# The last eight value blocks of the last attention head, as products of 32 stationary columns

## The chip, the cores and the metric

One core of one Trainium2 chip runs the whole program. The metric is the device time of one execution in microseconds. The kernel before takes 385.89 us, the median of 3 runs that lie between 385.88 and 386.0 us.

## The reference, cut to what matters

A decode step of one transformer block for 4 requests. A layer norm modulated by a condition feeds grouped-query attention over a cache of 4096 positions: 32 query heads on 8 key/value heads, so that 4 query heads share each cache. The result is projected, added to the input under a gate, normed and modulated again, and passes through a token-mixing MLP. All is 32-bit floating point.

```python
h = layernorm(x) * (1 + ca) + sa
q = (h @ wq).reshape(B, 1, 32, 128)             # B = 4 requests, one token each
scores = einsum("bhqd,bhkd->bhqk", q, k) / sqrt(128)
o = einsum("bhqk,bhkd->bhqd", softmax(scores), v)
x = x + ga * (o.reshape(B, 1, 4096) @ wo)
h = layernorm(x) * (1 + cb) + sb
x = x + gb * mixer_mlp(h)                       # w1, gelu, w2 over the token axis
```

## The kernel before, in words

The 4 requests times 8 key/value heads make 32 *heads*, numbered 0 to 31. Each has 2 MB of keys and 2 MB of values. One queue, SP's, loads them in order into a ring of three buffers; weights are loaded between them.

For each head the kernel forms the scores on TensorE, takes their maximum, exponentiates them on ScalarE, turns the result in 32 by 32 blocks on VectorE, and multiplies it with the values. The values of a head are 32 *blocks* of 128 positions by 128 channels. The turned weights `pT[:, j, :]` of block `j` are 32 columns, of which columns 0, 8, 16 and 24 belong to the four query heads and the others are padding.

A product on TensorE has a stationary operand, which is loaded first, and a moving operand, which streams through. In 32 bits each product is issued as two pairs of a weight load and a matmul. A stationary operand of 32 columns uses one of four *column groups* of the array, chosen by which 32 partitions of PSUM it writes; four products on the four groups can be under way together.

For the last heads `values_narrow` (line 294) takes the 32 weight columns as the stationary operand and a block of 128 channels as the moving one, block `j` on group `j % 4`. This leaves four partial sums in `pve`, query heads in rows and channels in columns. `copy_v` (line 311, step V31) brings them to SBUF as `po`, and `pick` (line 318, step a31) multiplies `po` with `eight`, a constant of four columns that adds the four groups, keeps the four real query heads and turns the result, so that channels lie on the partitions and the four heads in columns (`OT`).

Head 31 is split. Its first 30 blocks go that way. For its blocks 30 and 31 `values_turned` (line 305, step z31) takes the values themselves as 128 stationary columns and the four real weight columns as the moving operand; this gives the turned sum without a selection, in the same PSUM tile to which `pick` then adds the other 30 blocks.

`copy_o` (line 331, step A31) multiplies the sum with the inverse softmax sums into `both`. `project` (line 337, step p31) multiplies it with the output weights into `pgx`. Step I, ahead of it on TensorE, adds the gated residual `ep` to the same tile by a product with the 128-column identity. Between the second and third query head of step p31 `mean_last` sums up `tally`, which step j has made on VectorE. What follows is one chain: mean, variance, norm, 14 slices of the MLP and the output.

From head 23 on the order of the steps on every engine is written out by hand in `PLAN` (line 731). A step's letters name a function, its number the head, the digit after the point a part. `LV31` loads head 31's values in the pieces of `cuts` (line 729): blocks 0 to 15, 16 to 23, 24 to 27, 28 and 29, 30 and 31. `v31.0` to `v31.3` multiply them as they land, in the parts of `last` (line 730). Step f between them is a VectorE product of another tile, and step LW loads the last 1 MB of modulation weights behind all values; `zw0` uses them near the end.

Of the kernel before, what the change touches and what calls it, by code (L numbers as in the profile page):

```python
# [8 lines left out]
F32 = mybir.dt.float32  # L9
# [6 lines left out]
REP = HQ // HKV  # L16
NF = F // 128
EPS = 1e-5
P = 128
NS = B * HKV  # L20
# [8 lines left out]
def adaln_decode(ctx: ExitStack, tc: tile.TileContext, small, x, wmod, wq, kk, kv, vv, wo, out):  # L29
# [9 lines left out]
    ps_m = ctx.enter_context(tc.tile_pool(name="ps_m", bufs=2, space=PSUM))  # L39
    ps_e = ctx.enter_context(tc.tile_pool(name="ps_e", bufs=1, space=PSUM))  # L40
    ctx.enter_context(tc.manual_schedule())
    mm = nc.tensor.matmul
# [44 lines left out]
    eight = g32.rearrange("p (r x) -> p r x", x=8)[:, :, 0]  # L87
# [69 lines left out]
    KT, VT, WM = {}, {}, {}  # L157

    def slots():
        return ring.tile([P, 2, SK], F32, name="kv", tag="kv")  # L160
# [29 lines left out]
    def load_wm5():  # L190
        t = slots().rearrange("p s (k n) -> p (s k) n", n=D)
        nc.sync.dma_start(t[:, 0:4], wmod[2][:, 1])
        WM[5] = t[:, 0:4]
        return t[:, 4:6]

    def load_key(t, i):
        nc.sync.dma_start(t, kv[i - 2][:, 0])
        key(t, i)

    def load_v(t, i, cuts):  # L200
        value(t, i)
        src = (kv[i][:, 1] if i < NS - 2 else vv[i - NS + 2]).rearrange("p (j d) -> p j d", d=DH)
        for lo, hi in zip(cuts, cuts[1:]):
            nc.sync.dma_start(VT[i][:, lo:hi], src[:, lo:hi])
# [58 lines left out]
    def turn(i, halves=None):  # L263

        S.pop(i, None)
        if halves is None:
            dv.transpose(PL[i][0], PL[i][0])  # L267
            return
        for n in halves:
            p = PL[i][0][:, n * 512:(n + 1) * 512]  # L270
            dv.transpose(p, p)
# [22 lines left out]
    def values_narrow(i, ks, pv=None):  # L294
        if ks[0] == 0:
            PV[i] = ps_v.tile([P, DH], F32, name="pvn", tag="pv") if pv is None else pv
        pv = PV[i]
        pT = PL[i][0].rearrange("p (k r) -> p k r", r=32)
        top = 32 if i < NS - 1 else 30
        for k in ks:  # L300
            for j in range(4 * k, min(4 * k + 4, top)):
                c = j % 4
                mm(pv[32 * c:32 * c + 32, :], pT[:, j, :], VT[i][:, j, :], start=(k == 0), stop=(j + 4 >= top))  # L303

    def values_turned(i):
        pT = PL[i][0].rearrange("p (k r) -> p k r", r=32)
        OT[i] = pt = ps_m.tile([P, REP], F32, name="pt", tag="m")
        for j in (30, 31):
            mm(pt, VT[i][:, j, :], pT[:, j, 0:32:8], start=(j == 30), stop=False)

    def copy_v(i):
        pv = PV[i]
# [3 lines left out]
    ACC, OT = {}, {}  # L316

    def pick(i):
        po = PV.pop(i)
        n, m = po.shape[-1] // DH, WIDE.get(i, 1)  # L320
        if i in OT:
            mm(OT[i], po, eight, start=False, stop=True)
            return
        pt = ps_m.tile([P, m, REP], F32, name="pt", tag="m")
        OT[i] = pt[:, 0]
        for c in range(n):
            sel = sel4[:, c, :] if n > 1 else eight
            mm(pt, po[:, c * DH:(c + 1) * DH], sel.unsqueeze(1).to_broadcast([P, m, REP]),  # L328
               start=(c == 0), stop=(c == n - 1))
# [7 lines left out]
    def project(i, pa=None, between=None):  # L337
        b, h = divmod(i, HKV)
        oT = OT[i]
        if pa is None:  # L340
            pa = ps_m.tile([P, D], F32, name="pa", tag="m")
            for g in range(REP):
                mm(pa[32 * g:32 * g + 32, :], oT[:, g:g + 1].to_broadcast([P, 32]), wo_t[h][:, g, :],  # L343
                   start=True, stop=True)
        else:
            for g in range(REP):
                for c in range(4):
                    mm(pa[32 * c:32 * c + 32, :], oT[:, g:g + 1].to_broadcast([P, 32]),  # L348
                       wo_t[h][:, g, c * P:(c + 1) * P], start=(g == 0 and h == HKV - 2),
                       stop=(g == REP - 1 and h == HKV - 1))  # L350
                if between and g == 1:
                    between()
        PA[i] = pa
# [9 lines left out]
    def fold_groups(pool, acc, tag):  # L363
        pc = pool.tile([P, P], F32, name="pc", tag=tag)
        for c in range(4):
            mm(pc[32 * c:32 * c + 32, :], first, acc[:, c * P:(c + 1) * P], start=True, stop=True)
        return pc
# [215 lines left out]
    def fold_gate(gate, es):  # L583
        for e in es:
            w = wo_t[HKV - 2 + e // REP][:, e % REP]
            dv.tensor_tensor_reduce(w, w, gate, 1.0, 0.0, OP.mult, OP.add, rowsum[:, e:e + 1])
# [33 lines left out]
    def squares(x):  # L620
        flat = wk.tile([P, P], F32, name="flat")
        nc.scalar.activation(flat, x, AF.Square, bias=mu, accum_out=sq)
# [57 lines left out]
    for i in range(NS - HKV):  # L680
# [30 lines left out]
        if i == 2:  # L711
            for t in range(2, 5):
                pm = mod(t)
                dst = prep[:, {2: 1, 3: 2, 4: 3}[t]]
# [12 lines left out]
    pve = pgx = pc = ep = spare = slot = None  # L727
    gates = list(range(2 * REP))
    cuts = {NS - 1: (0, 16, 24, 28, 30, 32), NS - 2: (0, 16, 32)}
    last, halves = [(0, 1, 2, 3), (4, 5), (6,), (7,)], [(0, 1), (2, 3), (4, 5), (6, 7)]  # L730
    PLAN = """
    a23 v24.0 A23 p23 t25.0 P23 F R v24.1 LP25 G s26 t25.1 M H V24 LP26 Q a24 S26 v25.0 N s27 x A24 f p24 g
    x LP27 m26 S27 P24 m27 X26 X27 b26 B26 e26 x b27 v25.1 c g t26.1 l25 t26.0 B27 s28 V25 c g L25
# [1 line left out]
    LK30 t27.1 S29 P26 v27.0 m29 l27 g LK31 T t28.1 X29 LT t28.0 s30 L27 S30 b29 v27.1 B29 e29 l28 m30 V27  # L735
    LV28 L28 a27 g X30 t29.1 t29.0 l29 L29 s31 A27 LV29 b30 p27 x B30 S31 c c m31 e30 P27 X31 v28.0 f LT LV30
    b31 v28.1 B31 f e31 LV31 l30 V28 L30 t30.1 l31 L31 a28 t31.1 A28 p28 v29.0 v29.1 t30.0 f P28 V29 v30.0 a29
    v30.1 A29 LW p29 f v30.2 v30.3 t31.0 P29 g V30 Y y a30 A30 p30 E x v31.0 f v31.1 v31.2 v31.3 V31 z31 a31 I A31 j zy p31
    g T2 za zs zr zc0 zp0 zq zg zp1 zm zc1 T3 zn zw0
    """  # L740
    TABLE = {"s": scores, "S": row_max, "m": turn_max, "X": col_max, "b": spread_max, "B": copy_max, "e": expo,
# [4 lines left out]
    for step in PLAN.split():  # L746
        op, k = step.rstrip("0123456789."), step.lstrip("abcdefghijklmnopqrstuvwxyzABCDEFGHIJKLMNOPQRSTUVWXYZ")
        i, q = (int(n) for n in (k + ".0").split(".")[:2]) if k else (0, 0)
        if op in TABLE:
            TABLE[op](i)  # L750
        elif op in MIX:
            MIX[op]()
        elif op == "t":
            turn(i, [q])
        elif op == "v":
            if i < NS - 2:
                (values if i < NARROW else values_narrow)(i, range(4 * q, 4 * q + 4))
                continue
            if i == NS - 2 and q == 0:
                pve = ps_s.tile([P, 8, P], F32, name="pve", tag="s")  # L760
            values_narrow(i, (last if i == NS - 1 else halves)[q], pve[:, 4 * (NS - 1 - i)])
        elif step == "z31":
            values_turned(i)
        elif op == "p":
            project(i, pgx[:, 4] if i >= NS - 2 else None, mean_last if i == NS - 1 else None)
        elif op == "LT":
            slot = slots()
        elif op == "LK":
            load_key(slot[:, i % 2], i)
        elif op == "LV":  # L770
            load_v(slot[:, i % 2], i, cuts.get(i, (0, 32)))
        elif op == "LW":
            spare = load_wm5()
        elif op == "x":
            mix.expand(spare if mix.n == 6 else None)
        elif op == "f":
            fold_gate(gate, gates[:1])
            del gates[:1]
        elif step == "T":
            nc.scalar.activation(tab, neg1, AF.Exp)  # L780
        elif op == "Y":
            pgx = ps_s.tile([P, 8, P], F32, name="pgx", tag="s")
        elif op == "y":
            pc = fold_groups(ps_m, ACC.pop(B - 1), "m")
        elif op == "E":
            ep = cst.tile([P, P], F32, name="ep")
            dv.tensor_mul(ep, pc, prep[:, 1])
            dv.tensor_tensor_reduce(ep, ep, prep[:, 0], g32[:, 8 * (B - 1):8 * (B - 1) + 1], 0.0, OP.add, OP.add,
                                    tally[:, 0:1])
        elif op == "I":  # L790
            mm(pgx[:, 4], ident, ep, start=False, stop=False)
        elif step == "T2":
            nc.scalar.activation(tab, ones[0:1, 0:1], AF.Sqrt)
        elif step == "T3":
            nc.scalar.activation(tab, neg1, AF.Gelu_apprx_tanh)
        elif op == "za":
            al = centre(pgx[:, 4])
        elif op == "zs":
            squares(pgx[:, 4])
        elif op == "zr":  # L800
            products(al)
        elif op == "zp":
            if i == 0:
                ph = ps_s.tile([P, D], F32, name="ph3", tag="s")
            spread_last(ph, al, range(2 * i, 2 * i + 2))
        elif op == "zc":
            mix.fold_rest(i)
        elif op == "zg":
            pg = moments()
        elif op == "zm":  # L810
            variance(pg)
        elif op == "zn":
            hb, wr, br = affine_last(ph)
        elif op == "j":
            tally_up()
        elif op == "zw":
            modmm(pgx[:, 0], 5, (0,))
# [36 lines left out]
```

## Time and profile before

| | |
|---|---|
| median of 3 runs | 385.89 us |
| profiled execution, its own time | 385.9 us |
| its span, from first to last instruction | 384.1 us |
| TensorE matmul busy | 290.1 us (76%) |
| VectorE busy | 199.4 us (52%) |
| ScalarE busy | 111.9 us (29%) |
| DMA queue of the loads, share of 16 engines | 95.5% |
| read from memory | 157.32 MB, 410 GB/s over the span |

The engines are PE (TensorE matmul), PEld (TensorE weight load), DVE (VectorE), ACT (ScalarE), POOL (GpSimd) and SP (SyncE, which here issues loads). A row of the timeline has a start in us from the beginning of the span, a length, the engine, the line of the kernel, the operation, the tile written and those read, the shapes, and how many instructions of this kind follow each other (x8). Brackets at its end tell how long the engine was idle before and what released it. The length of a merged row goes from the first start to the last end. Ends of matmuls are modelled.

### The profile page before, as it was taken

What the parts mean: (1) busy time and instruction counts of PE and PEld (TensorE: products, weight loads), DVE (VectorE), ACT (ScalarE), POOL (GpSimd) and SP (SyncE); (2) the same over time, 40 slices, a digit from 0 to 9 for tenths busy, and PEclk for the clock granted to TensorE, in tenths of its full rate; (3) what the DMA queues carried; (4) which work ended last, traced back from release to release, by engine and by line L of the source; (5) the groups of instructions that cost most, each with busy time, mean ns of one, the idle gap of its engine ahead of it and who ended that gap; (6) DMA issues with size and microseconds to landing.
All of it is one profiled execution on the core that took longest, in us unless ns stands there. A gap on an engine that the chain in (4) does not pass through costs nothing.

```text
span 384.1 us, 5670 instructions
## 1 busy us (share of the span) xinstructions
PE 290.1 (76%) x2412; PEld 117.2 (31%) x2412; DVE 199.4 (52%) x414; ACT 111.9 (29%) x143; POOL 9.0 (2%) x34
## 2 busy tenths in 40 slices
PE   0958484973855928798777879988887887889984
PEld 0112121320222302234222223342222344333673
DVE  0130531440442714556666544657665567778777
ACT  1001210121110111113457310214675104757266
POOL 2100000000000000000000000000000000000000
PEclk9979956697896979989999995999999999999999
DMA  8999999999999999999999999999999999999930
GB/s 332 437 437 437 403 459 427 411 440 433 421 439 437 435 437 433 432 433 432 427 428 433 433 427 432 433 435 437 437 428 430 432 432 431 416 431 426 417 142 4
DMA packets 7410, 157.70 MB, mean 411 GB/s; under 512 B 964, under 2 KB 1236, under 8 KB 1496
## 3 DMA queue, kind: packets, MB, share of 16 engines
q1 hardware_dynamic: 7376, 157.33, 95.5%
q8 instruction: 19, 0.31, 0.3%
q14 instruction: 7, 0.06, 0.0%
q10 hardware_dynamic: 8, 0.00, 0.0%
HBM read 157.32 MB, written 0.01 MB: 410 GB/s over the span
## 4 chain that ended last, share of the span: by engine, by line
DMA 60%; PE 29%; DVE 8%; ACT 2%; issue 1%; POOL 0%; SPq 0%; DVEq 0%; ACTq 0%
DMA kv<-in_kv 58%; PE s L231 7%; PE pv L291 7%; PE s L122 3%; PE qs L138 2%; DVE p L267 2%; DVE m L236 2%; DMA sm<-in_small 2%; PE pa L343 2%; PE pt L328 2%; ACT wo L556 1%; PE pb L251 1%; PE pve L303 1%; PE pm L240 1%; PE pgx L348 1%
## 5 line engine op out<-in xcount | busy, mean ns | idle before, releaser
L231 PE MATMUL s<-kv,QT 128*32 128x512 f32 x512 | 71.8, 685 | 48.7 <-DMA kv<-in_kv 48.4
L236 DVE TENSOR_REDUCE m<-s 128x1 f32<-128x1024 f32 x32 | 39.2, 1224 | 100.7 <-PE s L231 100.7
L261 ACT ACTIVATE p<-s,nm 128x1024 f32<-128x1024 f32 x32 | 35.6, 1114 | 181.2 <-DVE nm L256 181.1
L291 PE MATMUL pv<-kv,p 128*32 128x512 f32 x464 | 67.8, 652 | 0.6 <-DMA kv<-in_kv 0.6
L231 PEld LDWEIGHTS s<-kv,QT 128*32 128x32 f32 x512 | 15.3, 119 | 91.0 <-DMA kv<-in_kv 62.9
L328 PEld LDWEIGHTS pt<-g,po 128*128 128x128 f32 x236 | 30.6, 202 | 27.6 <-issue 20.3
L343 PE MATMUL pa<-wo,oT 128*32 128x512 f32 x240 | 33.7, 633 | 4.9 <-DVE oT L335 4.7
L328 PE MATMUL pt<-g,po 128*128 128x4 f32 (+2 forms) x236 | 33.4, 265 | 1.5 <-DVE po L314 1.0
L267 DVE STREAM_TRANSPOSE p<-p 128x1024 f32<-128x1024 f32 x25 | 30.9, 1235 | 0.0
L314 DVE COPY po<-pv 128x512 f32<-128x512 f32 x29 | 20.0, 689 | 15.7 <-PE pv L291 15.6
L245 DVE TENSOR_REDUCE mx<-pm 1x128 f32<-1x512 f32 x32 | 21.3, 669 | 0.9 <-PE pm L240 0.9
L428 DVE TENSOR_SCALAR u<-hb,wr,sm 128x512 f32<-128x512 f32 x40 | 19.9, 540 | 1.9 <-POOL wr L423 1.0
L485 ACT ACTIVATE u<-u 128x1024 f32<-128x1024 f32 x20 | 20.4, 1052 | 1.5 <-DVE u L428 1.4
L261 ACT ACT_TABLE_LOAD x11 | 14.1, 1283 | 21.9 <-DVE nm L256 21.8
L361 DVE TENSOR_TENSOR acc<-acc,pa 128x512 f32<-128x512 f32 x26 | 17.8, 686 | 2.2 <-PE pa L343 2.1
L251 PEld LDWEIGHTS pb<-neg,mx 1*128 1x128 f32 x64 | 10.0, 194 | 27.6 <-DVE mx L245 25.9
L122 PE MATMUL s<-wm,sT 128*4 128x512 f32 x16 | 9.9, 788 | 10.4 <-POOL sT L108 10.4
L485 ACT ACT_TABLE_LOAD x13 | 16.7, 1283 | 0.2
L291 PEld LDWEIGHTS pv<-kv,p 128*32 128x32 f32 x464 | 13.6, 146 | 6.8 <-issue 2.8
L240 PE MATMUL pm<-ident,m 128*1 128x128 f32 x32 | 8.9, 280 | 7.6 <-DVE m L236 3.5
L251 PE MATMUL pb<-neg,mx 1*128 1x1 f32 x64 | 12.7, 265 | 2.1 <-DVE mx L245 2.1
L240 PEld LDWEIGHTS pm<-ident,m 128*1 128x1 f32 x32 | 2.5, 80 | 34.6 <-DVE rl L280 25.6
(173 smaller groups left out, 227.6 us busy)
## 6 DMA issues: line engine op xcount, KB each, us to landing
kv<-in_kv SPq DMA_DIRECT2D x28, 4096.0 KB, 22.0
wq<-in_wq SPq DMA_DIRECT2D x2, 4096.0 KB, 16.1
wo<-in_wo SPq DMA_DIRECT2D x4, 2048.0 KB
kv<-in_kv SPq DMA_DIRECT2D x4, 2048.0 KB, 21.1
wm<-in_wmod SPq DMA_DIRECT2D x2, 2048.0 KB, 16.1
kv<-in_kk SPq DMA_DIRECT2D x1, 4096.0 KB
kv<-in_vv SPq DMA_DIRECT2D x3, 1024.0 KB
wm<-in_wmod SPq DMA_DIRECT2D x1, 1024.0 KB
```

The lines of the kernel that those rows point to most:

```text
L122: mm(s0[0:B, t * D:(t + 1) * D], sT[:, k, :], wm01[:, t, k, :], start=(k == 0), stop=(k == 3))
L231: mm(s[32 * c:32 * c + 32, n * 512:(n + 1) * 512], QT[:, b, h, :], KT[i][:, (n * 4 + c) * 512:(n * 4 + c + 1) * 512], start=True, stop=True)
L236: dv.tensor_reduce(M[i], S[i], axis=AX.X, op=OP.max)
L245: dv.tensor_reduce(mx, M[i].rearrange("o (c r) -> o r c", c=4).unsqueeze(1).to_broadcast([1, 4, 32, 4]), axis=AX.X, op=OP.max)
L251: mm(pb, M[i].rearrange("o c r -> o (c r)"), neg1, start=True, stop=True)
L261: nc.scalar.activation(p, S[i], AF.Exp, bias=M.pop(i), accum_out=l)
L267: dv.transpose(PL[i][0], PL[i][0])
L291: mm(PV[i][32 * q:32 * q + 32, :], pT[:, 128 * k:128 * k + 128:4], VT[i][:, 4 * k:4 * k + 4, :].rearrange("p j d -> p (j d)"), start=(k < ...
L314: dv.tensor_copy(PV[i], pv)
L328: mm(pt, po[:, c * DH:(c + 1) * DH], sel.unsqueeze(1).to_broadcast([P, m, REP]), start=(c == 0), stop=(c == n - 1))
L343: mm(pa[32 * g:32 * g + 32, :], oT[:, g:g + 1].to_broadcast([P, 32]), wo_t[h][:, g, :], start=True, stop=True)
L485: nc.scalar.activation(u, u, AF.Gelu_apprx_tanh)
```

## The change

Head 31's narrow products now stop at block 23 instead of 29. Blocks 24 to 31 go through `values_turned`, and no longer with 128 stationary columns: each block's values are cut into four quarters of 32 channels, one for each column group, by the new function `quarters`. The four moving columns and the turned result stay as they were. The selection in `pick` is cut into quarters in the same way. In the order of steps the copy of the partial sums, V31, stands right behind the products of block 23. Then follow, all on TensorE, the products of blocks 24 to 27 (z31.0), the selection (a31), blocks 28 and 29 (z31.1), and blocks 30 and 31 (z31.2); step I and the rest follow as before. The loads and their pieces are unchanged.

```diff
-        top = 32 if i < NS - 1 else 30
+        top = 32 if i < NS - 1 else 24
...
-    def values_turned(i):
+    def quarters(dst, lhs, rhs, start, stop):
+        for c in range(4):
+            mm(dst[32 * c:32 * c + 32], lhs[:, 32 * c:32 * c + 32], rhs, start=start, stop=stop)
+
+    def values_turned(i, js):
         pT = PL[i][0].rearrange("p (k r) -> p k r", r=32)
-        OT[i] = pt = ps_m.tile([P, REP], F32, name="pt", tag="m")
-        for j in (30, 31):
-            mm(pt, VT[i][:, j, :], pT[:, j, 0:32:8], start=(j == 30), stop=False)
+        if js[0] == 24:
+            OT[i] = ps_m.tile([P, REP], F32, name="pt", tag="m")
+        for j in js:
+            quarters(OT[i], VT[i][:, j, :], pT[:, j, 0:32:8], j == 24, j == 31)
...
         if i in OT:
-            mm(OT[i], po, eight, start=False, stop=True)
+            quarters(OT[i], po, eight, False, False)
...
-    last, halves = [(0, 1, 2, 3), (4, 5), (6,), (7,)], [(0, 1), (2, 3), (4, 5), (6, 7)]
+    last, halves = [(0, 1, 2, 3), (4, 5)], [(0, 1), (2, 3), (4, 5), (6, 7)]
...
-    ... E x v31.0 f v31.1 v31.2 v31.3 V31 z31 a31 I A31 j zy p31
+    ... E x v31.0 f v31.1 V31 z31.0 a31 z31.1 z31.2 I A31 j zy p31
...
-        elif step == "z31":
-            values_turned(i)
+        elif op == "z":
+            values_turned(i, {0: range(24, 28), 1: (28, 29), 2: (30, 31)}[q])
```

More of the change, by code (lines that the diff above doesn't have):

```diff
@@ L737, in adaln_decode @@
     b31 v28.1 B31 f e31 LV31 l30 V28 L30 t30.1 l31 L31 a28 t31.1 A28 p28 v29.0 v29.1 t30.0 f P28 V29 v30.0 a29
-    v30.1 A29 LW p29 f v30.2 v30.3 t31.0 P29 g V30 Y y a30 A30 p30 E x v31.0 f v31.1 v31.2 v31.3 V31 z31 a31 I A31 j zy p31
+    v30.1 A29 LW p29 f v30.2 v30.3 t31.0 P29 g V30 Y y a30 A30 p30 E x v31.0 f v31.1 V31 z31.0 a31 z31.1 z31.2 I A31 j zy p31
     g T2 za zs zr zc0 zp0 zq zg zp1 zm zc1 T3 zn zw0
```

## The prediction

> **What bounds the kernel now.** I read the page first, for what sets the end at large.
>
> ```profile
> span 384.1 us, 5670 instructions
> DMA 60%; PE 29%; DVE 8%; ACT 2%; issue 1%; POOL 0%; SPq 0%; DVEq 0%; ACTq 0%
> q1 hardware_dynamic: 7376, 157.33, 95.5%
> ```
>
> The loads fill their queue nearly to the end, and the change touches none. So all it can win or lose lies between the landing of head 31's last values and the end, and I turned to the timeline there (stretches of it, by engine):
>
> ```profile
> 365.46 1.58 PEld L303 LDWEIGHTS pve<-kv,p 128*32 128x32 f32 x56
> 365.57 2.05 PE L303 MATMUL pve<-kv,p 128*32 128x128 f32 x60
> 366.14 0.69 DVE L586 CUSTOM_DVE_ANT_0 wo<-wo,gate 128x512 f32<-128x512 f32 x1
> 367.21 0.14 PEld L303 LDWEIGHTS pve<-kv,p 128*32 128x32 f32 x4 [0.17 <-DMA kv<-in_vv]
> 367.67 0.29 DVE L314 COPY po<-pve 128x128 f32<-128x128 f32 x1 [0.83 <-PE pve L303]
> 367.68 0.52 PEld L309 LDWEIGHTS pt<-p,kv 128*128 128x128 f32 x4 [0.33 <-PE pve L303]
> 367.71 0.58 PE L309 MATMUL pt<-p,kv 128*128 128x4 f32 x4
> 368.15 0.36 PE L322 MATMUL pt<-g,po 128*128 128x4 f32 x2
> 368.34 0.30 PEld L791 LDWEIGHTS pgx<-ep,ident 128*128 128x128 f32 x2
> 368.37 0.47 PE L791 MATMUL pgx<-ep,ident 128*128 128x128 f32 x2
> 368.55 0.16 DVE L335 TENSOR_TENSOR both<-pt,rl 128x4 f32<-128x4 f32 x1 [0.59 <-PE pt L322]
> 368.77 0.38 PEld L348 LDWEIGHTS pgx<-wo,both 128*32 128x32 f32 x16
> ```
>
> Blocks 0 to 23 run without a pause, as do 24 to 27 behind them; for blocks 28 and 29 TensorE waits for their piece until 367.21. For the last piece the instructions of line 309 have a row:
>
> ```profile
> L309 PE MATMUL pt<-p,kv x4: 245/252/253, 367.7 to 368.0; 128*128 128x4 f32 x4
> L309 PEldq EVENT_SEMAPHORE  x1: 51/51/51, 367.6 to 367.6; - x1
> ```
>
> TensorE's sequencer waits there, and the first product of block 30 follows at 367.68. The row names another releaser (the products of line 303, ended at 365.57 + 2.05 = 367.62), but this wait, done at about 367.65, is the later of the two. So the last values are there at **about 367.6**, and from then on everything is a chain on engines: 0.58 us of turned products, the selection until 368.15 + 0.36 = 368.51, step A31, and the projection at 368.77. The chain of waits tells what follows:
>
> ```profile
> 368.51 0.33 PE pgx L791 x2
> 368.84 0.56 PE pgx L348 x14
> 369.98 0.37 DVE a L617 x2
> 381.35 0.29 DVE osb L571
> ```
>
> All of it to the end hangs on the projection's first weight load, at 368.77. I cost the change by where this load goes.
>
> **The change part by part.** *The pace of four-group products* is the price on which all hangs, since 12 + 4 + 2 = 18 instructions become none, and instead eight blocks and a selection cost 9 x 4 x 2 = 72. The nearest row is `mean_last`, 32 stationary columns on four groups, with one moving column:
>
> ```profile
> 369.12 0.24 PEld L668 LDWEIGHTS pmu<-part,tally 128*32 128x32 f32 x8
> 369.23 0.22 PE L668 MATMUL pmu<-part,tally 128*32 128x1 f32 x8
> L668 PE MATMUL pmu<-part,tally x8: 167/168/170, 369.2 to 369.3; 128*32 128x1 f32 x8
> 369.26 0.38 PEld L348 LDWEIGHTS pgx<-wo,both 128*32 128x32 f32 x16
> ```
>
> Eight products of 0.17 us each end within 0.22, so they start within 0.05 of each other, 7 ns apart. A group's loads go ahead once the products of the group before have started: those of line 668's second group at 369.23, those of the next step (line 348) at 369.26. So a group of four costs **0.03 us**. The other bound is the pace with 128 moving columns:
>
> ```profile
> 365.46:366.87 1.41, 1.30 (x48) 1.33 (x48) 1.00 0.93 361
> ```
>
> This is line 303 alone in that window: 48 matmuls and loads, the loads busy for 1.33; a load takes 0.11 (next fence), so the 12 groups start (1.33 - 0.13)/11 = 0.11 us apart. I take 0.03, since four moving columns are nearer to one than to 128; the range keeps both.
>
> *The copy V31* moves ahead. Block 23's loads start at about 366.66 (11 groups of 0.11 after 365.46), its products one group later, at 366.79 with the four in a row, and they end 0.27 after (the length of a line 303 product, below), at 367.06. The copy came 0.05 after the end of its products (367.62, 367.67): now 367.11 to **367.40**. DVE is free, since line 586 ends at 366.83; were it not, the selection and the end would come as much later.
>
> ```profile
> L303 PEld LDWEIGHTS pve<-kv,p x60: 106/110/110, 365.5 to 367.2; 128*32 128x32 f32 x60
> L303 PE MATMUL pve<-kv,p x60: 272/273/297, 365.6 to 367.3; 128*32 128x128 f32 x60
> 363.68 0.29 DVE L314 COPY po<-pve 128x128 f32<-128x128 f32 x1 [0.33 <-PE pve L303]
> 364.03 0.30 PEld L328 LDWEIGHTS pt<-g,po 128*128 128x128 f32 x2 [0.46 <-DVE po L314]
> ```
>
> *z31.0.* Blocks 24 to 27 were multiplied right at 366.87 (the window holds exactly 24 blocks' 48 loads), so their piece was there. The step opens the tile `pt` and may need the extra wait instruction of line 309: start by 366.94. Eight groups of 0.03 end at 367.18, hidden behind the copy (0.52 until the selection can start, so up to 0.06 a group); without that cover the 0.24 would be on the path.
>
> *a31* is where a wait is added: it stands ahead of the last eight groups, and z31.1, z31.2, I and the projection queue behind it on TensorE. A selection loads 0.06 after its copy (363.97, 364.03): 367.46. Two groups: 367.52. *z31.1*, whose values came by 367.21, needs four groups, to 367.63; *z31.2*, whose values came at 367.6, four more: its last products start at **367.75** and, at 0.17 each, end at 367.92. The copy's path and the last load's (367.62 + 0.10) thus meet within 0.03; neither leaves room for more.
>
> *A31* started 0.04 after its products' end (368.51, 368.55), and the projection's load 0.22 after that: 367.96 and **368.18**. By this path alone 0.59 would be won.
>
> *Step I*, unchanged, comes into the way. It has 128 stationary columns between products of 32, and where the width changes, the trace shows loads that wait for no one else and yet start late:
>
> ```profile
> 298.78 0.43 PE L366 MATMUL pc<-yw,g 128*32 128x128 f32 x8 [0.83 <-DVE yw L501]
> 299.14 0.97 PEld L578 LDWEIGHTS pgb<-prep,ident 128*128 128x128 f32 x8 [0.20 <-issue]
> 371.37 0.69 PE L632 MATMUL ph<-a,ident 128*128 128x128 f32 x4
> 371.99 0.16 PEld L516 LDWEIGHTS pc<-u,sm 128*32 128x32 f32 x8
> ```
>
> Each starts 0.07 before the modelled end of the product ahead (299.21 and 299.14; 372.06 and 371.99). Before, this change of width lay ahead of block 30, under the wait for the last piece; now it lies ahead of I: its load starts at 367.92 - 0.07 = 367.85 (before, I came at the full pace of 0.11 behind the selection). From I's first load to the projection's were 368.77 - 368.34 = 0.43 us, and that too was bound by I: its products end at 368.84, 0.07 after. So the projection can load at **368.28**, 0.10 after `both` is ready. The wait moves from the selection to I.
>
> The sum: 368.77 - 368.28 = **0.49 us**. Behind it nothing has a fixed time that comes late. ACT's table is loaded by 368.82, before its use at 370.37 - 0.49; the last weights, issued at 357.69, land 12.3 later, at 370.0, before their use at 372.56 - 0.49.
>
> ```profile
> 357.69 0.33 SPq L192 DMA_DIRECT2D kv<-in_wmod  x1
> kv<-in_wmod SPq DMA_DIRECT2D x1, 1024.0 KB, 12.3
> 368.62 0.20 ACT L793 ACTIVATE tab<-ones 1x1 f32<-1x1 f32 x1
> 370.37 0.37 ACT L622 ACTIVATE flat<-pgx,mu 128x128 f32<-128x128 f32 x1 [1.55 <-DVE a L617]
> 372.56 0.24 PEld L209 LDWEIGHTS pgx<-kv,sT 128*32 128x32 f32 x8
> ```
>
> The profiled execution took 385.9 us, 1.8 more than its span, and the runs' median is the same 385.89: I forecast **385.4 us**, 385.2 to 385.6 with the roundings.
>
> **The rivals.** *The products are issued at 0.11 a group (slower).* The mechanism: each small product holds the array's entry for its own quarter of what a full one holds, whatever its moving columns. For it speaks line 309, also with four moving columns: four products in 0.58, 0.25 of it the last one's length, are 0.11 apart. Against it, that these have 128 columns to load, and line 668. Then z31.0 ends at 367.82, past the copy; ten groups more put the last products at 368.81 + 0.11, and the projection 0.53 later (0.17 - 0.07 + 0.43): 369.45, a loss of 0.68, **386.6 us**. It decides from a pace of 0.07 a group on: there the last products start at 368.24 and the projection at 368.77.
>
> For the same rival stands the Trainium skill, TensorEngine Tiling (Array Packing), section Instruction Overhead: every matmul carries about 60 cycles, so a small dimension is no place to gain by tiling; at the 2.4 GHz of its page TensorE: Matmul & The Clock Gate I estimate 25 ns a product, 0.10 a group, a loss of about 0.5 and 386.4. Line 668's products, 7 ns apart across four groups, disagree.
>
> *Half pace.* Line 668 shows only two groups in a row; over ten, load and product of a group could alternate instead of overlapping, 0.03 each: 0.06 a group, so the last products start at 368.03 and the projection at 368.56: a gain of 0.2, **385.7 us**. For it speaks only that no longer run is in the trace.
>
> *I does not wait for the array to empty,* as it did not behind the selection: then A31's path holds, 0.59, **385.3 us**. Against it are both rows on the change of width.
>
> *It is hidden anyway,* by something in the tail that keeps its own time: **385.9 us**. The rows of ACT and of the last weights speak against it, with 0.5 and 1.8 us of room.
>
> **How the numbers follow.** Forecast 0.58; no emptying ahead of I 0.12; half pace 0.10; hidden 0.07; 0.11 or 0.10 a group 0.10; something not seen 0.03. The largest gain that the last landing allows is 0.6 us, 0.16%, and 0.2%, about what a measurement of this kernel can tell from no change, is 0.77 us: all cases lie within it. Over it, at 385.1, I put 0.11 for a build whose loads end earlier by chance; below, beyond 386.7, 0.07, mostly from the slow pace. Within: 0.82. The range runs from 385.1 to 386.3: it takes in the forecast, the small rivals and the slow pace up to 0.09 a group; left out are its far end and the luck at either side.
>
> **What would show it.** Right: the copy at line 314 starts near 367.1; 32 loads of the turned products come ahead of the selection within 0.25; the last turned products start 0.1 to 0.2 after the last piece's landing; line 335 some 0.6 earlier against that landing; line 348 released by I and not by `both`, 0.5 earlier. Wrong: turned products 0.1 apart by group; a selection that waits on the copy past 367.5; an idle stretch ahead of line 348 that names DVE; a tail of other length than 15.3 us from line 348's first load to the end of the span.

## The result, and the profile after

| | before | after |
|---|---|---|
| median | 385.94 us (4 runs, 385.88 to 386.04) | 389.63 us (4 runs, 389.09 to 390.12) |
| ratio | | 1.0096, 95% interval 1.0081 to 1.0111 |
| profiled execution, span | 385.9, 384.1 us | 390.12, 388.3 us |

The change makes the kernel slower by about 1%, 3.7 us, where 0.5 us less was forecast. The profiled execution is the slowest of the four, so its profile accounts for 4.2 us and not for 3.7. The stretch that I had costed went nearly as forecast; the time was lost behind it. First the timeline of the changed kernel around the change (line numbers are 5 higher than before from line 314 on):

```profile
366.87 0.38 PEld L307 LDWEIGHTS pt<-p,kv 128*32 128x32 f32 x32 [0.15 <-issue]
367.05 0.29 DVE L319 COPY po<-pve 128x128 f32<-128x128 f32 x1 [0.29 <-PE pve L303]
367.40 0.16 PEld L307 LDWEIGHTS pt<-g,po 128*32 128x32 f32 x8 [0.15 <-DVE po L319]
367.45 0.37 PEld L307 LDWEIGHTS pt<-p,kv 128*32 128x32 f32 x32
367.85 0.30 PEld L796 LDWEIGHTS pgx<-ep,ident 128*128 128x128 f32 x2
367.98 0.16 DVE L340 TENSOR_TENSOR both<-pt,rl 128x4 f32<-128x4 f32 x1 [0.63 <-PE pt L307]
368.26 0.38 PEld L353 LDWEIGHTS pgx<-wo,both 128*32 128x32 f32 x16
368.75 0.16 PEld L353 LDWEIGHTS pgx<-wo,both 128*32 128x32 f32 x7
371.88 0.39 PEld L353 LDWEIGHTS pgx<-wo,both 128*32 128x32 f32 x9 [2.97 <-issue]
```

The projection's first load comes at 368.26, 0.51 earlier than before. But within its second half, after seven of sixteen loads, TensorE stands still for 2.97 us, and the profile names nothing that it waits for: "issue". The chain of waits has it on the path:

```profile
368.94 0.24 PE pgx L353 x7
369.18 2.70 issue
371.89 0.85 PE pgx L353 x9
```

Two sets of windows cut the end at the same instructions: the loads of head 30's projection, the first load of step p31, the load that comes late after the change, the first slice of the MLP (line 551, now 556), the end. The columns are the window, its length, busy time with instruction counts of PE, PEld, DVE, ACT and POOL, granted clock, share and GB/s of DMA. Before:

```profile
364.67:368.77 4.10, 4.01 (x101) 3.40 (x101) 2.59 (x10) 2.49 (x3) 0.00 (x0) 1.00 0.80 325
368.77:369.31 0.54, 0.54 (x29) 0.54 (x31) 0.54 (x3) 0.05 (x1) 0.00 (x0) 1.00 0.29 121
369.31:373.27 3.96, 3.71 (x88) 3.05 (x80) 2.97 (x14) 2.20 (x5) 0.76 (x2) 1.00 0.04 12
373.27:384.10 10.83, 5.04 (x136) 3.28 (x136) 8.07 (x19) 7.21 (x7) 0.00 (x0) 1.00 0.02 4
```

After:

```profile
364.59:368.26 3.67, 3.60 (x154) 3.23 (x154) 2.65 (x10) 2.07 (x2) 0.00 (x0) 1.00 0.83 333
368.26:371.88 3.62, 0.92 (x32) 0.65 (x31) 0.91 (x4) 0.48 (x2) 0.00 (x0) 0.90 0.17 70
371.88:377.47 5.59, 5.58 (x61) 4.81 (x65) 2.53 (x12) 2.20 (x5) 0.76 (x2) 0.50 0.01 3
377.47:388.30 10.83, 7.01 (x152) 4.72 (x144) 8.08 (x19) 7.21 (x7) 0.00 (x0) 0.82 0.02 4
```

Up to step p31: -0.51 (368.26 against 368.77), of which 0.08 was there before the change could act (head 30's projection at 364.59 against 364.67). The stretch with the pause: 3.62 for 0.54, +3.08. The norm behind it: 5.59 for 3.96, +1.63, at a granted clock of 0.50 instead of 1.00. The MLP and the output: 10.83 both times; in both kernels the chain runs through ScalarE for the first 6.7 us of it. The sum, +4.20, is the difference of the spans, 388.3 - 384.1.

What the pause waits for is told by the queues. The page counts q8, a queue of instructions, with 19 packets and 0.31 MB in both kernels: 16 KB each. Divided among them, TensorE's 2 x 2412 matmuls and loads of before are 254 a packet, so 256 instructions a packet is a likely size. In the changed kernel's DMA view, q8 moves nothing between 366 and 369.5 us, while the loads (q1) run; then comes one packet (columns: queue, packets, MB, share of 16 engines in a window of 0.1 us from 369.5 on):

```profile
q8 instruction: 1, 0.02, 58.8%
```

2.3 us later TensorE goes on, at 371.88. That made the **supply theory**: TensorE's instructions arrive in pieces of 256; the change has it use up one piece sooner than the next is there. Its rivals: the pause belongs to the place (step p31's second half, or the sums it needs; the *place theory*), to the turned products or to the new order.

### The profile page after: what moved, and what is told of

The parts are those of the page before. It is cut to its first block, busy times and chain, and to the rows that moved or that the text cites. A ratio compares the mean times of both kernels' runs of the same rounds, so it can differ in the third digit from the quotient of the medians.

```text
span 388.3 us, 5778 instructions
## 1 busy us (share of the span) xinstructions
PE 294.4 (76%) x2466; PEld 119.7 (31%) x2466; DVE 199.3 (51%) x414; ACT 111.9 (29%) x143; POOL 9.0 (2%) x34
## 4 chain that ended last, share of the span: by engine, by line
DMA 60%; PE 27%; DVE 8%; ACT 2%; issue 1%; POOL 0%; SPq 0%; ACTq 0%; DVEq 0%
DMA kv<-in_kv 58%; PE s L231 7%; PE pv L291 6%; PE s L122 3%; DVE m L236 3%; PE qs L138 2%; DVE p L267 2%; DMA sm<-in_small 2%; ACT wo L561 1%; PE pa L348 1%; PE pt L333 1%; PE pb L251 1%; PE pve L303 1%; PE pgx L353 1%; PE pm L240 1%
## 5 line engine op out<-in xcount | busy, mean ns | idle before, releaser
L291 PE MATMUL pv<-kv,p 128*32 128x512 f32 x464 | 66.5, 640 | 0.6 <-DMA kv<-in_kv 0.6
L348 PE MATMUL pa<-wo,oT 128*32 128x512 f32 x240 | 32.8, 618 | 5.0 <-DVE oT L340 4.8
L433 DVE TENSOR_SCALAR u<-hb,wr,sm 128x512 f32<-128x512 f32 x40 | 19.9, 540 | 1.9 <-POOL wr L428 1.0
```

The costliest lines, as they stand in the source:

```text
L291: mm(PV[i][32 * q:32 * q + 32, :], pT[:, 128 * k:128 * k + 128:4], VT[i][:, 4 * k:4 * k + 4, :].rearrange("p j d -> p (j d)"), start=(k < ...
```

## The experiments

Where a run is said to be shifted, products that make the first row of `prep` are repeated with the same result at the start of the program. Each is four instructions of TensorE, two loads and two matmuls:

```diff
+    for e in range(16):
+        c = e % 4
+        mm(px[32 * c:32 * c + 32, :], rows.rearrange("k b r -> k (b r)"),
+           xr[:, c * P:(c + 1) * P], start=True, stop=True)
```

### The changed kernel, shifted by 64 instructions

> The changed kernel, with 16 more of the small products that make the first row of prep (line 153, repeated, same result) at the start, where TensorE waits for loads: 64 instructions more ahead of everything that follows, nothing else. Supply theory: TensorE's instructions arrive in pieces of 256, and the pause of 2.97 us begins where a piece ends; then it begins 64 instructions earlier, at step I, ahead of the first load of step p31 and not within its second half; it still ends near 371.3 to 371.9 us, and the time stays at 389 to 390.5 us. Place theory: the pause belongs to step p31's second half (what it reads, or the sums that line 673 makes); then it stays between the seventh and the eighth load there, and the time at 389.6 us.

389.82 us (4 runs), ratio 1.0102 (1.0076 to 1.0127). The pause moved 64 instructions forward, to the middle of step I, in which no sum of step p31 is needed:

```profile
367.79 0.19 PEld L800 LDWEIGHTS pgx<-ep,ident 128*128 128x128 f32 x1
370.98 0.19 PEld L800 LDWEIGHTS pgx<-ep,ident 128*128 128x128 f32 x1 [3.00 <-issue]
```

A window from the start of the span to a moment within the pause counts what TensorE has begun by then. For the changed kernel:

```profile
0.00:371.00 371.00, 281.77 (x2261) 110.17 (x2261) 188.73 (x383) 102.51 (x131) 8.27 (x32) 0.91 0.99 425
```

For the shifted one:

```profile
0.00:370.00 370.00, 280.50 (x2261) 110.27 (x2261) 188.47 (x382) 102.64 (x131) 8.26 (x32) 0.92 0.99 426
```

Both stop after exactly **2261 matmuls and 2261 loads** (4522 instructions; the 4545 of the expectations counts 23 waits and the like with them). The place theory falls.

### The kernel before, shifted by 108 instructions

> The kernel before, with 27 more of the small products that make the first row of prep at the start: 108 instructions more, as many as the change adds, but none of the change. Supply theory: the piece that ended at 372.36 us in the kernel before now ends 108 instructions earlier, in the second half of step p31 at about 369.4 us, and the next is there some 5.8 us after the piece before it was finished (about 364.8): a pause of about 1.2 us, between 0.7 and 1.6, and a time of 386.7 to 387.6 us without the change. Place theory, or any cause that lies in the turned products themselves: no pause, 385.9 us.

386.45 us (10 runs), ratio 1.0021 (1.0008 to 1.0034). None of the change is in it, and there is a pause at the same count, now in step p31:

```profile
369.80 0.25 PEld L352 LDWEIGHTS pgx<-wo,both 128*32 128x32 f32 x9 [0.60 <-issue]
```

```profile
0.00:369.70 369.70, 288.96 (x2261) 112.61 (x2261) 188.56 (x383) 102.64 (x131) 8.27 (x32) 0.89 1.00 426
369.80:374.00 4.20, 3.63 (x69) 2.97 (x69) 2.92 (x13) 2.56 (x6) 0.76 (x2) 1.00 0.03 8
```

It is half as long as the 1.2 us expected, below my 0.7, the clock behind it stays at 1.00 (second row), and the loss of 0.5 us is below my range too. So a pause needs neither the turned products nor the new order; the products at the start, far from the end, cost time at the end.

### The changed kernel, shifted by 148 instructions

> The changed kernel with 37 more of the small products at the start: 148 instructions, so that with the change's 108 the ends of pieces are 256 further on, one of them again where it was in the kernel before, in step zc1 behind the norm. Supply theory: the pause within step p31 is gone; one piece ends at the border of z31.0 and the selection, near 367.4 us, with a pause of 1 to 2 us there; the next end lies in zc1, where TensorE has time; 386.4 to 387.6 us. Place theory: the pause of 3 us stays in step p31, 389.6 us.

The profiled execution took 387.44 us, inside the expectation; its pause was where expected, one product short of the selection, again after 2261 loads:

```profile
369.26 0.11 PEld L311 LDWEIGHTS pt<-p,kv 128*32 128x32 f32 x1 [1.95 <-issue]
```

```profile
0.00:368.50 368.50, 295.87 (x2261) 116.46 (x2261) 187.91 (x378) 102.26 (x130) 8.27 (x32) 0.87 1.00 427
369.26:374.00 4.74, 4.69 (x135) 4.17 (x139) 3.21 (x16) 1.77 (x4) 0.33 (x1) 1.00 0.05 16
```

Over the six runs, though, the median is 389.37 (387.44, 387.86, and four from 389.11 to 390.52), outside it. The second row shows a full clock behind this pause. The slower four lie 1.7 to 3.1 us above it. A halved clock alone (1.63 us in the changed kernel) would fit only the nearest of them, and they were not profiled: what they lost stays open.

### The new order alone

The function `quarters` makes one product of full width, so that the number of instructions is that of the kernel before:

```diff
     def quarters(dst, lhs, rhs, start, stop):
-        for c in range(4):
-            mm(dst[32 * c:32 * c + 32], lhs[:, 32 * c:32 * c + 32], rhs, start=start, stop=stop)
+        mm(dst, lhs, rhs, start=start, stop=stop)
```

> The new order of steps alone: blocks 24 to 31 as turned products and the copy ahead of them, but with 128 stationary columns, and the selection in one product: the number of TensorE's instructions is that of the kernel before. Supply theory: no pause in step p31, as the pieces end where they ended before; ten products pairs of 0.22 us each put the projection's first load near 369.4 us, 0.6 later than before: 386.3 to 386.7 us. Theory that the new order makes the pause: 3 us of it remain, 389 us or more.

The profiled execution, at 386.46 us, is as expected: no pause, and the projection at 369.32.

```profile
368.00 0.97 PEld L306 LDWEIGHTS pt<-p,kv 128*128 128x128 f32 x8
369.32 0.38 PEld L352 LDWEIGHTS pgx<-wo,both 128*32 128x32 f32 x16
```

So the order makes no pause, and four groups of 32 columns are worth 1.06 us here (369.32 - 368.26). Over ten runs the median is 387.42 (386.44 to 391.37; ratio 1.0043, 1.0017 to 1.0068), outside the expectation; what the slower half of them lost was not seen in a profile and stays open.

### Four turned blocks, and the same with zc0 late

Blocks 24 to 27 go back to narrow products, the copy stands behind them and the selection is last: 60 instructions more than before instead of 108. In the second run step zc0, 32 instructions that fold another request's sums, is moved behind the norm.

```diff
-        top = 32 if i < NS - 1 else 24
+        top = 32 if i < NS - 1 else 28
...
-    ... f v31.1 V31 z31.0 a31 z31.1 z31.2 I A31 j zy p31
-    g T2 za zs zr zc0 zp0 zq zg zp1 zm zc1 T3 zn zw0
+    ... f v31.1 v31.2 V31 z31.0 z31.1 a31 I A31 j zy p31
+    g T2 za zs zr zp0 zq zg zp1 zm zc0 zc1 T3 zn zw0
```

> The run with four turned blocks, with zc0 left where it was. Supply theory: instruction 4545 now is one of the last of zc0, wanted near 369.6 us, and the pause begins there and ends near 371.9, 2 to 2.4 us long; 387 us if TensorE keeps its clock, up to 389 us if the pause halves it. Rival, that the number of turned products or the order of copy and products makes the pause: no pause with zc0 at either place, or the same in both.

> The change with four instead of eight turned blocks (28 to 31), the copy behind block 27, the selection last, and step zc0 (32 instructions of TensorE that fold another request's sums, not needed at once) moved from behind step p31 to just ahead of zc1. 60 instructions more than the kernel before, but the piece's end (4545 of TensorE's instructions in the trace) now falls into zc0 behind the norm, wanted near 371.5 to 371.9 us, when the next piece is there (about 371.9). Supply theory: no pause on the path; the projection's first load comes at about 368.3 us, 0.46 earlier than before, and the time is 385.3 to 385.7 us. If four-group turned products cost time in another way than by the supply: 386 us or more, or a pause at another place.

With zc0 in its place: 387.8 us (4 runs), ratio 1.0056 (1.0043 to 1.0069), and the pause at the count of 2261, within zc0's last products:

```profile
371.79 0.13 PEld L521 LDWEIGHTS pc<-u,sm 128*32 128x32 f32 x1 [2.32 <-issue]
```

```profile
0.00:371.00 371.00, 285.77 (x2261) 113.27 (x2261) 189.80 (x389) 102.97 (x133) 8.27 (x32) 0.90 0.99 425
```

With zc0 late: 385.54 us (12 runs), beside 385.96 for the kernel before. The one profiled execution, at 387.03, had its work come 1.6 us late from before head 31 on, so the same kernel was run again:

> The same kernel as the run with four turned blocks and zc0 late, since the one execution of it that was profiled was one whose work came 1.6 us late from before head 31 on. Supply theory: an ordinary profile shows no pause, the projection's first load about 0.75 us after the last piece's landing (1.19 before), a tail of 15.35 us behind it, and 385.4 to 385.6 us.

385.56 us (12 runs, one of them at 883.34 us and not in the ratio below), beside 385.93 of before. The profile shows no pause and the projection at 368.36; the window from there to the end has the 15.34 us that it has before (384.1 - 368.77 = 15.33).

```profile
368.36 0.38 PEld L353 LDWEIGHTS pgx<-wo,both 128*32 128x32 f32 x16
```

```profile
368.36:383.70 15.34, 9.42 (x237) 7.00 (x236) 11.58 (x35) 9.94 (x14) 0.77 (x2) 0.97 0.05 19
```

So a cut of the change that keeps the path's gain, and lets the piece end where TensorE has time, undoes the loss: about 0.4 us lies between the medians, twice. There is little to spare: the packet came at 369.39, so by the 2.3 us the next piece was there at about 371.7 (an estimate), and TensorE wanted it at 371.72. As ratios with their intervals, 0.9993 (0.9985 to 1.0001) and 0.9999 (0.9987 to 1.0010), neither is shown to be faster, since each set holds one or two executions at 387 us; nine of the eleven that the second comparison uses lie below the fastest of before's 17.

### The kernel before with zc0 late

> The kernel before with step zc0 moved ahead of zc1 and nothing else: what of the run with four turned blocks comes from this move. Supply theory: no pause before or after, since the norm's wait hides zc0 in either place: 385.8 to 386.0 us. Rival: zc0 late delays the last products of the MLP, 386.2 to 386.5 us.

385.96 us beside 385.96, ratio 1.0013 (0.9992 to 1.0033): the move alone is worth nothing. Its worth above is that of where it puts the end of the piece.

### The changed kernel with a short last load

```diff
-        nc.sync.dma_start(t[:, 0:4], wmod[2][:, 1])
-        WM[5] = t[:, 0:4]
+        nc.sync.dma_start(t[:, 0:1], wmod[2][:, 1, 0:1])
+        WM[5] = t[:, 0:1].to_broadcast([P, 4, D])
```

> The changed kernel with a quarter of the last load: of the last 1 MB of modulation weights only the first 256 KB are loaded and used for all four quarters (it leaves out three quarters of that load). The loads then end near 368.2 us instead of 370.0. In the changed kernel the piece of instructions was finished at 366.15, the transfer of the next began at 369.54, while loads still ran, and the first instruction of it came at 371.88. If the transfer waits for its turn behind the loads, it begins by about 368.3, and the pause ends near 370.6: 1.7 us long instead of 2.97, and 387.5 us or so. If its lateness has another cause, it begins near 369.5 all the same and the pause stays at 2.9 to 3 us.

386.43 us (9 runs), ratio 1.0011 (0.9999 to 1.0022). The kernel leaves out three quarters of the last weights, so its output is not that of the block; it shows only where the time goes. About 3 us of the loss are gone with a load that nothing on the path waits for. The transfer of the piece comes in the 0.1 us from 367.6 on, 1.9 earlier, and the pause is shorter:

```profile
q8 instruction: 1, 0.02, 59.3%
```

```profile
368.86 0.16 PEld L353 LDWEIGHTS pgx<-wo,both 128*32 128x32 f32 x7
369.95 0.25 PEld L353 LDWEIGHTS pgx<-wo,both 128*32 128x32 f32 x9 [0.93 <-issue]
```

```profile
0.00:369.80 369.80, 286.34 (x2261) 112.13 (x2261) 188.81 (x383) 102.49 (x131) 8.27 (x32) 0.89 0.99 424
369.95:374.00 4.05, 3.62 (x69) 2.96 (x69) 2.77 (x13) 2.41 (x6) 0.76 (x2) 1.00 0.01 4
```

So the transfer waits behind the loads. From its start to the next instruction it is again 2.3 us (369.95 - 367.65), as in the changed kernel (371.88 - 369.55). The gain is larger than the pause alone, since the clock stays at 1.00: from the late load to the first slice of the MLP it is 3.84 us here (373.79 - 369.95), against 5.59 at a clock of 0.50 in the changed kernel.

```profile
373.79 1.52 ACT L556 ACTIVATE wo<-hb,br,wr 128x512 f32<-128x512 f32 x2 [0.19 <-DVE br L663]
```

### The changed kernel, shifted by 256 instructions

> The changed kernel with 64 more of the small products at the start, 256 instructions: one whole piece. Supply theory, with pieces of 256: the ends of pieces fall where they fell in the changed kernel, and the pause is back between the seventh and eighth load of step p31's second half, some 3 us long, 389 to 390.5 us; it begins at 4801, 256 more than the 4545 at which it began in every run that had one. If the place depended on the amount shifted and not on the piece, the pause would be gone or elsewhere.

389.82 and 387.79 us (2 runs): the first, which was profiled, inside the expectation, the second below it. The pause is back in step p31 between the seventh and the eighth load, at a count of 2389 of each, which is 2261 + 128:

```profile
371.89 0.24 PEld L357 LDWEIGHTS pgx<-wo,both 128*32 128x32 f32 x9 [2.03 <-issue]
```

```profile
0.00:371.00 371.00, 290.12 (x2389) 115.46 (x2389) 188.74 (x383) 102.64 (x131) 8.26 (x32) 0.90 0.99 425
371.89:377.50 5.61, 5.61 (x65) 4.90 (x69) 2.82 (x13) 2.50 (x6) 0.76 (x2) 0.53 0.01 3
```

The piece is 256 instructions. The pause is a microsecond shorter than expected, as everything ahead of it came some 0.9 later in this execution.

### Four turned blocks, step I in quarters

```diff
-            mm(pgx[:, 4], ident, ep, start=False, stop=False)
+            quarters(pgx[:, 4], ident, ep, False, False)
```

> The run with four turned blocks and zc0 late, with step I cut into quarters of 32 columns too (12 instructions more) and 244 instructions of small products at the start, so that pieces end 12 earlier and 256 later: where they ended in that run. Supply theory and the reading of step I: no change of width ahead of the projection any more, which then starts by the sum's path, 0.05 to 0.1 us earlier than with step I in full width; 385.3 to 385.6 us. If the shift were not right, a pause would show at the piece's end, 386 us or more.

386.62 us (11 runs, one of them at 664.52 us and not in the ratio), ratio 1.0018 (1.0009 to 1.0028), outside the expectation. There is no pause, and the projection is released by `both` as expected, no longer by step I. But head 31's values landed later; the wait for blocks 24 to 27 ended at 368.26:

```profile
368.26 0.16 PEld L307 LDWEIGHTS pve<-kv,p 128*32 128x32 f32 x8 [0.26 <-DMA kv<-in_vv]
369.63 0.16 PEld L357 LDWEIGHTS pgx<-wo,both 128*32 128x32 f32 x8 [0.31 <-DVE both L344]
```

The profiled execution of the shift by 256 had late values too. From issue to landing the last two pieces took 19.9 us here and 19.3 in the shift by 256, against 18.4 in the kernel before; in the shifts by 64, 108 and 148 they took 17.2, 17.5 and 18.4. So not every shift delays them, and why these two do stays open.

What a narrow step I is worth on the path, the rows still tell, if counted from the selection's first load. Here are the selection and step I of the last run with four blocks, where step I has 128 columns, and of this one, where it has 32:

```profile
367.77 0.16 PEld L307 LDWEIGHTS pt<-g,po 128*32 128x32 f32 x8
367.95 0.30 PEld L796 LDWEIGHTS pgx<-ep,ident 128*128 128x128 f32 x2
```

```profile
369.10 0.16 PEld L311 LDWEIGHTS pt<-g,po 128*32 128x32 f32 x8
369.15 0.16 PEld L311 LDWEIGHTS pgx<-ep,ident 128*32 128x32 f32 x8
```

Behind the same eight products the load of step I comes 0.18 us after the selection's first in full width and 0.05 us in quarters. The projection's comes after 0.59 (368.36) and 0.53 us (369.63): 0.06 us are gained, as expected.

## Why the prediction failed

**The step that failed** is the sentence behind the sum: "Behind it nothing has a fixed time that comes late." I had checked the activation table and the last weights, and not the next 256 instructions. They have such a time: the transfer came at 369.5 and could be used from 371.88 on. In the kernel before the same transfer came in the 0.1 us from 369.3 on, so its instructions were there at about 371.7 (an estimate by the same 2.3 us). TensorE wanted the first of them, after 4522 loads and matmuls, at 372.36, 0.7 us later:

```profile
q8 instruction: 1, 0.02, 58.5%
```

```profile
0.00:366.13 366.13, 278.30 (x2131) 108.38 (x2135) 186.61 (x375) 99.97 (x128) 8.27 (x32) 0.91 1.00 428
0.00:372.36 372.36, 284.39 (x2259) 113.47 (x2263) 190.50 (x394) 104.01 (x135) 8.32 (x33) 0.91 0.99 423
```

The change brought that moment to 368.9, for two reasons: 0.5 us of gain on the path, and 108 instructions more, which put an end of a piece that had lain behind the norm into step p31. The kernel before shifted by 108 has the second reason without the first, and paused for 0.60 us; the gain alone would have brought the moment only to about 371.9 (372.36 - 0.51), when by the estimate the piece was there. My rival "hidden anyway" named the right place, something in the tail that keeps its own time, but had no price beyond the lost gain, 385.9, and a chance of 0.07. The room that it gave the two things it did check is summed wrongly: by its own rows it is 1.1 us for ACT (369.88 - 368.82) and 2.1 for the last weights (372.07 - 370.0), not 0.5 and 1.8; nothing hangs on that.

**What the 72 matmuls cost** (each with a load, so 72 for 18 makes 108 instructions more) I had asked only of the array. There the answer was right: the turned products ran at about 0.04 us a group where I had taken 0.03 (32 loads of 0.11 in 0.37: (0.37 - 0.11)/7), and the slow pace, for which the Trainium skill's rule stood too (TensorEngine Tiling (Array Packing), section Instruction Overhead), did not occur. Their price as instructions to be fetched I put at nothing, though the page of before has the packets, 19 of 16 KB. With the norm's wait among them, the kernel before had taken 6.2 us for the 256 that end at 372.36 (the first row above counts 256 fewer, at 366.13). The changed kernel uses as many in 2.8 us, from 366.06 to 368.9:

```profile
0.00:366.06 366.06, 278.71 (x2132) 107.76 (x2136) 186.58 (x375) 99.97 (x128) 8.27 (x32) 0.91 1.00 428
```

**The halved clock** was in none of my cases: 1.63 us of the 4.20, on a stretch that took 3.84 us at full clock in the run with the short last load.

**What was right**, each against its forecast: the copy at 367.05 (367.11); the selection's load at 367.40 (367.46); line 340 at 367.98 (367.96); step I's load at 367.85 (367.85), so that the projection hung on I and not on `both`; the projection's load at 368.26 (368.28). That the last agrees to 0.02 is in part luck: head 30's projection was 0.08 early in this execution, and from the selection's load to step I's it took 0.45 us, 0.06 more than forecast. TensorE shows no wait for the last piece either, so whether the last load's path would have met the copy's, as the sum has it, is not shown. The rivals on this stretch, slow pace, half pace and no emptying ahead of I, all fall with these rows. The range, 385.1 to 386.3, was built from them alone, and so held no case in which a stretch further on gets worse. Among the signs of being wrong, "a tail of other length than 15.3 us" is the one that showed: it is 388.3 - 368.26 = 20.0.

## What to carry to other kernels

Count an edit's instructions as well as their time. TensorE here used 256 short instructions in 2.8 us, while loads filled the DMA engines and the next piece was usable only 5.8 us after the piece before it was used up (366.06 to 371.88). Where a piece ends depends on every instruction ahead of it in the program. An idle stretch put down to "issue", in the midst of equal instructions, that comes at the same instruction count when the program is shifted, was that stall here. Before a path is made faster, see what it runs into: moving a step that nobody waits for behind the norm took away a pause of 2.32 us, and a shorter load ahead of the transfer cut one from 2.97 to 0.93 us.

## What the runs showed of the hardware that I had not expected

- TensorE's instructions come in pieces of 256. Seven kernels paused, six at exactly 2261 matmuls and 2261 loads, the seventh at 128 more of each after a shift by 256. The three kernels with 256 or more instructions beyond the kernel before (256, 316 and 364) have 20 packets on q8, all others 19. The Trainium skill, Runtime: NRT & Kernel Launch, section Instruction fetch mechanics, gives the blocks of 16 KiB and 256 instructions, which these runs confirm; that crossing a block's end is mostly hidden does not hold at this one, with 0.60 to 3.00 us in the open.
- The transfer of a piece waits behind loads: with three quarters of the last load left out it began 1.9 us earlier (367.6 against 369.5). It need not wait for their end: in the changed kernel shifted by 64 it came at 368.61, while loads ran until about 370.9. In all seven kernels that paused, TensorE went on 2.2 to 2.4 us after the start of the packet. What asks for it the trace does not name. From the moment the piece before was used up (some 4266 matmuls and loads begun), it came after 3.5 us in the changed kernel (366.06 to 369.54) and 1.7 us with the short load (366.00 to 367.67).
- A pause of TensorE can cost more than itself. Behind pauses of 2.03, 2.32, 2.97 and 3.00 us the granted clock was 0.5 for some microseconds; behind 0.60, 0.93 and 1.95 us it stayed at 1.00. That is one profile of each kernel, and the length of a pause was not varied by itself. Here are the windows behind the pauses of 3.00 us (a mean of 0.60, since the clock fell within it) and 2.32 us:

```profile
370.98:375.20 4.22, 4.22 (x65) 3.70 (x65) 1.12 (x7) 0.49 (x3) 0.00 (x0) 0.60 0.02 4
```

```profile
371.79:378.50 6.71, 6.63 (x69) 5.14 (x73) 3.97 (x12) 4.15 (x6) 0.76 (x2) 0.50 0.01 4
```

- Where products of 32 columns are followed by one of 128, the next load starts late, as the rows of the kernel before had shown: step I's came 0.06 us before the modelled end of the last turned product (367.85, and 367.48 + 0.43 = 367.91). With step I in quarters of 32 columns it came 0.13 us sooner behind the selection (0.05 against 0.18 us).
